# Half-row projections in pairs, two-bank PSUM tiles and a new step order in a linear-attention and gated-MLP kernel

## The chip, the cores and the metric

The kernel runs on one core of a Trainium2 chip. The metric is the device time of one launch in microseconds (us). TensorE (PE) multiplies matrices into PSUM, an accumulator of 8 banks (512 float32 values in each of 128 partitions); VectorE (DVE) and ScalarE (ACT) read PSUM and write SBUF; GpSimd (POOL) works on SBUF; SP and POOL issue most of the transfers.

## The reference

Inputs are q, k and v of 8 batches, 8 heads, 576 tokens and 64 values, and a projection w_phi of 64x128. For each head:

```python
def phi(x):
    proj = np.einsum('bhsd,df->bhsf', x, w_phi)
    proj = proj - np.max(np.abs(proj), axis=-1, keepdims=True)
    return np.concatenate([np.exp(proj), np.exp(-proj)], axis=-1)
q_p, k_p = (phi(q), phi(k))
kv = np.einsum('bhsf,bhsd->bhfd', k_p, v)
z = np.sum(k_p, axis=2)
num = np.einsum('bhsf,bhfd->bhsd', q_p, kv)
den = np.einsum('bhsf,bhf->bhs', q_p, z)[..., None] + 1e-06
```

The first stage gives num / den, a 576x512 matrix x per batch. The second stage multiplies x by w_in (512x1024), applies a relu and splits the result into u and v; v is normalized along its 512 values, mixed over tokens by the 576x576 matrix w_spatial, with a bias; u times the mixed v goes through w_out (512x512) to the output.

## The kernel before, in words

**Units and steps.** The 576 tokens are cut into 512 main tokens and a tail of 64. A unit is a pair of heads over the main tokens of one batch (32 pair units), or the tails of two batches over all 8 heads (4 tail units). Either way a unit is 128 partitions by 8 blocks. The Python loop at the end runs 40 steps for 36 units. In each step it emits, in the order of the table ORDER, pieces of first-stage work for units of different age (LAGS): keys of this step's unit, queries of the same one, attention of the unit three steps back, sums of the unit two back, and so on. After each piece, `fill(share)` adds RATE x share to a credit (in us of matmul) and takes as many second-stage tasks from a queue as the credit allows. What is left in the queue after the last step is emitted at the end. The tasks of a batch enter the queue when its last pair unit has passed the piece "out". Transfers are placed in the same loop, by unit numbers. Each engine runs its own instructions in the order they were given; waits are put in by the framework, also between two engines that read one PSUM bank.

**Projections.** `kT` and `qT` hold two blocks of 64 rows each, one under the other in 128 partitions. `wphi2` is a block-diagonal 128x256 matrix of two copies of w_phi and zeros, so `by_token` (L229 to L234) projects both blocks by one matmul of 256 columns, two of them to a PSUM bank. `a_keys` (L236) takes the maximum of the absolute values over each bank on VectorE (L244), then two exponentials of 512 columns on ScalarE (L247), with signs plus and minus; the maxima are applied by `a_scale`, which scales v on POOL (L272). `a_queries` (L249) takes maxima (L258) and splits them into a high and a low bf16 part in columns 0 to 15 of a 128x128 tile (L261, L262).

**Features.** `a_max_t` transposes that tile (L293, L294). `a_qfeat` (L296) projects the queries again, with the features on the partitions (L304 for pair units, L313 for tails), and subtracts each token's maximum by an accumulating matmul with a selector (L308, L315); two exponentials per bank follow (L321).

**Sums and numerators.** `a_kv` (L334, L336) multiplies key features by scaled v for two heads into one bank, which ScalarE or VectorE copies (L339). `a_num` (L354) multiplies query features by these sums into two banks; VectorE takes a reciprocal (L344) and multiplies (L345). `tail_num` (L382) does it for the tails in tiles of 64 columns.

**Second stage.** Tasks of four or five matmuls of 512 columns into one bank: v (L403, read by L405 on ScalarE and L406 on VectorE), u (L456, read by L458), the spatial mix (L477 and L478, read by L480 on VectorE), the output (L500, read by L502), and forms of them for the tails (L468, L489, L491).

**PSUM.** One pool of eight one-bank tiles serves everything: `psum = ... tile_pool(name="psum", bufs=8, ...)` at L57.

Of the kernel before, what the change touches and what calls it, by code (L numbers as in the profile page):

```python
# [8 lines left out]
FP32 = mybir.dt.float32  # L9
# [7 lines left out]
def kernel(  # L17
# [15 lines left out]
    nc = tc.nc  # L33
# [23 lines left out]
    psum = ctx.enter_context(tc.tile_pool(name="psum", bufs=8, space=bass.MemoryType.PSUM))  # L57
# [66 lines left out]
    wphi2 = cpool.tile([P, 2 * F], BF16)  # L124
    pin(nc.vector.memset)(wphi2, 0.0)
# [14 lines left out]
    sel1 = cpool.tile([P, H], BF16)  # L140
    sel = cpool.tile([P, H, F], BF16)
    pin(nc.vector.tensor_tensor)(out=sel1, in0=ident[:, 0:H], in1=ident[:, H:2 * H], op=ALU.add)
    pin(nc.vector.tensor_scalar)(out=sel, in0=sel1.unsqueeze(2).to_broadcast([P, H, F]), scalar1=-1.0,
# [4 lines left out]
    for i in range(2):  # L148
# [3 lines left out]
        if i == 0:  # L152
            for y in range(2):
                r = slice(y * D, (y + 1) * D)
                pin(nc.scalar.copy)(out=wphi2[r, y * F:(y + 1) * F], in_=wphi_f[r, :])
# [73 lines left out]
    def by_token(xT, half):  # L229
        ps = psum.tile([P, 4, F], FP32, tag="bank", name="ps")  # L230
        for x in range(2):
            nc.tensor.matmul(out=ps[:, 2 * x:2 * x + 2, :], lhsT=xT[:, 2 * half + x, :], rhs=wphi2,  # L232
                             start=True, stop=True)
        return ps  # L234

    def a_keys(u):  # L236

        u["mk"] = small.tile([P, H], FP32, tag="mk", name="mk")
        u["kf"] = feat.tile([P, 2, H, F], BF16, tag="kf" if u["pair"] else "kf_t", name="kf",
                            bufs=4 if u["pair"] else 2)  # L240
        for half in range(2):
            pk = by_token(u["kT"], half)
            hs = slice(4 * half, 4 * half + 4)
            nc.vector.tensor_reduce(out=u["mk"][:, hs], in_=pk, axis=AX.X, op=ALU.max,  # L244
                                    apply_absolute_value=True)
            for s, sc in ((0, 1.0), (1, -1.0)):
                nc.scalar.activation(out=u["kf"][:, s, hs, :], in_=pk, func=AF.Exp, bias=0.0, scale=sc)  # L247

    def a_queries(u):  # L249

        m, early = mhl[u["i"] % NM], u["i"] < EARLY
        if not early:
            mq = small.tile([P, H], FP32, tag="mq", name="mq")
        for half in range(2):
            pq = by_token(u["qT"], half)
            if early and half == 0:
                mq = pq[:, 0, 0:H]
            nc.vector.tensor_reduce(out=mq[:, 4 * half:4 * half + 4], in_=pq, axis=AX.X, op=ALU.max,  # L258
                                    apply_absolute_value=True)
        eng = nc.vector if early else nc.gpsimd  # L260
        eng.tensor_copy(out=m[:, 0:H], in_=mq)  # L261
        eng.tensor_tensor(out=m[:, H:2 * H], in0=mq, in1=m[:, 0:H], op=ALU.subtract)  # L262
# [28 lines left out]
    def a_max_t(u):  # L291
        pt = psum.tile([P, P], BF16, tag="bank", name="pt")
        nc.tensor.transpose(out=pt, in_=mhl[u["i"] % NM], identity=ident)  # L293
        nc.vector.tensor_copy(out=mT[u["i"] % NM][0:2 * H, :], in_=pt[0:2 * H, :])  # L294

    def a_qfeat(u):  # L296

        m = mT[u["i"] % NM]
        u["qf"] = []
        for half in range(2):  # L300
            pq = psum.tile([P, 4, P], FP32, tag="bank", name="pq")
            if u["pair"]:
                for par in range(2):
                    nc.tensor.matmul(out=pq[:, 2 * par:2 * par + 2, :], lhsT=wphi2[:, par * F:(par + 1) * F],  # L304
                                     rhs=u["qT"][:, 2 * half:2 * half + 2, :], start=True, stop=False)
                    for x in range(2):
                        j = 4 * half + 2 * x + par
                        nc.tensor.matmul(out=pq[:, 2 * par + x, :], lhsT=sel[:, j, :], rhs=m,  # L308
                                         start=False, stop=(x == 1))
# [374 lines left out]
```

## Time and profile before

| What | Value |
|---|---|
| median of 3 runs | 292.17 us (291.98 to 296.22) |
| span of the profiled execution, first to last instruction | 286.4 us |
| PE busy | 261.6 us, 91% |
| ACT busy | 229.3 us, 80% |
| DVE busy | 201.8 us, 70% |
| POOL busy | 182.2 us, 64% |
| TensorE clock granted | full throughout |
| HBM | 32.85 MB read, 9.44 MB written |

The profiled execution has no time of its own beside its span; the runs' median is 5.8 us above it, for what lies before the first and after the last instruction. The costliest groups are the exponentials of the keys (144 of 128x512, mean 692 ns) and of the features (128 for pairs, 675 ns), the scaling of v on POOL (64, 1049 ns), and the maxima of keys and queries (72 and 62 on VectorE, some 680 ns). A mean counts an instruction from start to end; where an engine starts the next one before the last has ended, starts lie closer together than that.

In the listings that follow, a line of the timeline has the start in us, the length of the run of like instructions in us, the engine, the line of the kernel, what is written and read, the tile of the array (rows*columns), the shape and the count. A line of the table by stretch has from:to, the length, the busy us and the count of each engine, the granted clock, the share of the DMA engines and GB/s.

### The profile page before, as it was taken

Reading aid. Unit: us, or ns where it says so; the run is one execution under the profiler, and the core shown is the slowest. Engines: PE = TensorE matmul, PEld = TensorE weight load, DVE = VectorE, ACT = ScalarE, POOL = GpSimd, SP = SyncE. Lnnn points to the kernel's source line nnn. Section 1 sums busy time; section 2 is a strip of 40 time slices with the busy share of each in tenths; the row PEclk is TensorE's granted clock in tenths of the full one; section 3 lists DMA queues with packets and bytes.
Section 4 is the critical chain, followed back from the end, with each engine's and each line's share of the span. In section 5 each row is a group of like instructions: output and inputs, shape, how many; then the busy total and the mean of one; then the engine's idle time right before and its main releaser. Section 6 shows DMA issues by size and latency. Waiting matters only on the chain.

```text
span 286.4 us, 7965 instructions
## 1 busy us (share of the span) xinstructions
PE 261.6 (91%) x3070; PEld 178.6 (62%) x3070; DVE 201.8 (70%) x509; ACT 229.3 (80%) x517; POOL 182.2 (64%) x320
## 2 busy tenths in 40 slices
PE   1378889999999999999989999999999999999983
PEld 1157776777666776767557687666667676545441
DVE  4389997977958877598696887578688864354610
ACT  4949998899799988999998679799999746566033
POOL 8159998798336899479689954835969600058200
PEclk9999999999999999999999999999999999999999
DMA  6989999976568499999955994999111003500037
GB/s 185 203 171 120 206 219 223 163 203 71 79 147 186 102 187 155 173 245 196 130 94 102 225 191 87 264 287 255 32 22 32 7 2 122 211 3 0 0 90 242
DMA packets 81706, 40.31 MB, mean 141 GB/s; under 512 B 50242, under 2 KB 77058, under 8 KB 81668
## 3 DMA queue, kind: packets, MB, share of 16 engines
q1 hardware_dynamic: 54180, 28.32, 43.0%
q0 software_dynamic: 27328, 11.41, 35.5%
q8 instruction: 24, 0.39, 0.6%
q14 instruction: 14, 0.11, 0.2%
q10 hardware_dynamic: 160, 0.07, 0.1%
HBM read 32.85 MB, written 9.44 MB: 148 GB/s over the span
## 4 chain that ended last, share of the span: by engine, by line
PE 61%; ACT 14%; DVE 11%; DMA 9%; POOL 2%; issue 2%; ACTq 0%; SPq 0%; POOLq 0%; DVEq 0%
PE pv L403 10%; PE ps L477 8%; PE po L500 7%; PE pu L456 7%; PE ps L232 5%; ACT qf L321 5%; ACT kf L247 5%; PE pv L334 4%; DMA q_tl<-in_q_dram 4%; PE pn L354 4%; DMA out_dram<-ob 3%; PE pq L308 3%; PE pq L304 3%; DVE mk L244 3%; PE ps L478 2%; DVE mq L258 2%
## 5 line engine op out<-in xcount | busy, mean ns | idle before, releaser
L247 ACT ACTIVATE kf<-ps 128x512 bf16<-128x512 f32 x144 | 77.7, 692 | 5.6 <-DVE mk L244 5.4
L272 POOL TENSOR_TENSOR vs<-v_f,em 128x512 bf16<-128x512 f32 x64 | 65.6, 1049 | 23.6 <-ACT em L267 22.6
L321 ACT ACTIVATE qf<-pq 128x512 bf16<-128x512 f32 x128 | 68.2, 675 | 8.5 <-PE pq L308 8.5
L244 DVE TENSOR_REDUCE mk<-ps 128x4 f32<-128x512 f32 x72 | 46.1, 677 | 2.5 <-PE ps L232 2.0
L258 DVE TENSOR_REDUCE mq<-ps 128x4 f32<-128x512 f32 x62 | 39.9, 681 | 4.2 <-PE ps L232 3.4
L502 ACT COPY ob<-po 128x512 f32<-128x512 f32 (+1 forms) x37 | 21.6, 610 | 19.9 <-PE po L500 16.2
L406 DVE BATCH_NORM_STATS2 stats<-vr 128x6 f32<-128x512 bf16 (+1 forms) x37 | 24.8, 687 | 15.8 <-ACT vr L405 15.7
L477 PE MATMUL ps<-w_spT,vn 128*128 128x512 bf16 x128 | 32.8, 379 | 0.0
L456 PE MATMUL pu<-xT,w_in_bf 128*128 128x512 bf16 x128 | 31.6, 379 | 0.0
L403 PE MATMUL pv<-w_in_bf,xT 128*128 128x512 bf16 x128 | 31.2, 379 | 0.0
L480 DVE TENSOR_TENSOR uT<-ps,uT 128x512 bf16<-128x512 f32 x32 | 22.0, 689 | 12.7 <-PE ps L478 11.5
L500 PE MATMUL po<-w_out_bf,uT 128*128 128x512 bf16 x128 | 30.4, 379 | 0.0
L308 PE MATMUL pq<-mT,sel 128*128 128x128 bf16 x256 | 30.0, 219 | 0.0
L308 PEld LDWEIGHTS <-sel 128*128 128x128 bf16 x256 | 25.1, 98 | 3.9
L405 ACT ACTIVATE vr<-pv 128x512 bf16<-128x512 f32 (+1 forms) x37 | 23.3, 691 | 4.0 <-PE pv L403 3.9
L354 PEld LDWEIGHTS <-qf 128*128 128x128 bf16 x512 | 20.4, 97 | 8.2 <-issue 1.7
L345 DVE TENSOR_TENSOR x<-pn,rc 128x256 bf16<-128x256 f32 x64 | 25.0, 418 | 0.5
L420 POOL TENSOR_SCALAR vn<-vr,rs 128x512 bf16<-128x512 bf16 x32 | 24.3, 773 | 0.8
L334 PE MATMUL pv<-vs,kf 128*128 128x66 bf16 x512 | 24.5, 194 | 0.2 <-ACT kf L247 0.2
L354 PE MATMUL pn<-kv,qf 128*128 128x66 bf16 x512 | 22.3, 193 | 1.3 <-ACT qf L321 1.2
L334 PEld LDWEIGHTS <-kf 128*128 128x128 bf16 x512 | 21.7, 97 | 1.8 <-issue 0.9
L304 PE MATMUL pq<-qT_b,wphi 128*128 128x256 bf16 x96 | 22.4, 273 | 0.0
(120 smaller groups left out, 530.8 us busy)
## 6 DMA issues: line engine op xcount, KB each, us to landing
v_f<-in_v_dram SPq DMA_DIRECT2D x8, 1024.0 KB, 10.7
out_dram<-ob SPq DMA_DIRECT2D x32, 256.0 KB, 3.6
k_bf<-in_k_dram POOLq DMA_DIRECT2D x7, 512.0 KB, 7.0
q_bf<-in_q_dram POOLq DMA_DIRECT2D x7, 512.0 KB, 8.7
v_tl<-in_v_dram SPq DMA_DIRECT2D x8, 128.0 KB, 7.7
w_in_bf<-in_moe_w_in_dram POOLq DMA_DIRECT2D x2, 512.0 KB, 8.7
out_dram<-ob SPq DMA_DIRECT2D x8, 128.0 KB, 2.4
k_tl<-in_k_dram POOLq DMA_DIRECT2D x8, 64.0 KB, 6.8
```

What stands on the lines that cost most here:

```text
L244: nc.vector.tensor_reduce(out=u["mk"][:, hs], in_=pk, axis=AX.X, op=ALU.max, apply_absolute_value=True)
L247: nc.scalar.activation(out=u["kf"][:, s, hs, :], in_=pk, func=AF.Exp, bias=0.0, scale=sc)
L258: nc.vector.tensor_reduce(out=mq[:, 4 * half:4 * half + 4], in_=pq, axis=AX.X, op=ALU.max, apply_absolute_value=True)
L272: nc.gpsimd.tensor_tensor(out=vs[:, s, :, 0:D], in0=st[u["b"]]["v"][:, pj * H:(pj + 1) * H, :], in1=em[:, s, :].unsqueeze(2).to_broadcast( ...
L308: nc.tensor.matmul(out=pq[:, 2 * par + x, :], lhsT=sel[:, j, :], rhs=m, start=False, stop=(x == 1))
L321: nc.scalar.activation(out=qf[:, s], in_=pq, func=AF.Exp, bias=0.0, scale=sc)
L334: nc.tensor.matmul(out=pv[:, hh, s, :], lhsT=u["kf"][:, s, 4 * hh + c, :], rhs=u["vs"][:, s, 4 * hh + c, :], start=(c == 0), stop=False)
L354: nc.tensor.matmul(out=pn[:, pos, :], lhsT=u["qf"][hh][:, s, pos, :], rhs=d["kv"][:, 2 * u["pj"] + hh, s, :], start=(s == 0), stop=(s == 1))
L403: nc.tensor.matmul(out=pv[r], lhsT=lhs(kc), rhs=w_in_bf[:, kc, HALF:DFF], start=(kc == 0), stop=(kc == KC - 1))
L456: nc.tensor.matmul(out=pu, lhsT=w_in_bf[:, kc, dc * P:(dc + 1) * P], rhs=d["xT"][:, kc, :], start=(kc == 0), stop=(kc == KC - 1))
L477: nc.tensor.matmul(out=ps, lhsT=d["vn"][:, sp, cs], rhs=w_spT[:, sp, 0:T0], start=(sp == 0), stop=False)
L500: nc.tensor.matmul(out=po[r], lhsT=lhs(dc), rhs=w_out_bf[:, dc, :], start=(dc == 0), stop=(dc == KC - 1))
```

## The change

PSUM is divided: a pool `wide` of two tiles of two banks, for keys and features, and a pool `psum` of four banks for everything else. The block-diagonal matrix is replaced by `wphi`, with w_phi in rows 0 to 63 and again in rows 64 to 127. Each projection is a matmul on 64 rows and 128 columns, emitted in pairs: the upper half to one bank, the lower half to the other. The blocks of a unit therefore stand in another order, which `slot` gives to the readers. Keys take one maximum over 1024 columns and two exponentials of 1024. Features take one pair of 512-column matmuls, then four pairs for the maxima; the maxima of the two halves are put into columns 0 to 7 and 64 to 71, and the selector has a copy for each half. The transposed maxima are copied on all 128 partitions. ORDER and RATE change: nothing is filled in between keys and queries, more after queries, sums and features; 3.7 us of matmul a step instead of 3.12.

```diff
-    psum = ctx.enter_context(tc.tile_pool(name="psum", bufs=8, space=bass.MemoryType.PSUM))
+    wide = ctx.enter_context(tc.tile_pool(name="wide", bufs=2, space=bass.MemoryType.PSUM))
+    psum = ctx.enter_context(tc.tile_pool(name="psum", bufs=4, space=bass.MemoryType.PSUM))
...
-    wphi2 = cpool.tile([P, 2 * F], BF16)
-    pin(nc.vector.memset)(wphi2, 0.0)
+    wphi = cpool.tile([P, F], BF16)
...
-    sel1 = cpool.tile([P, H], BF16)
-    sel = cpool.tile([P, H, F], BF16)
-    pin(nc.vector.tensor_tensor)(out=sel1, in0=ident[:, 0:H], in1=ident[:, H:2 * H], op=ALU.add)
-    pin(nc.vector.tensor_scalar)(out=sel, in0=sel1.unsqueeze(2).to_broadcast([P, H, F]), scalar1=-1.0,
+    sel1 = cpool.tile([P, 4], BF16)
+    sel = cpool.tile([P, 4, F], BF16)
+    pin(nc.vector.tensor_tensor)(out=sel1, in0=ident[:, 0:4], in1=ident[:, 4:8], op=ALU.add)
+    for i in (D, D + 4):
+        pin(nc.vector.tensor_tensor)(out=sel1, in0=sel1, in1=ident[:, i:i + 4], op=ALU.add)
+    pin(nc.vector.tensor_scalar)(out=sel, in0=sel1.unsqueeze(2).to_broadcast([P, 4, F]), scalar1=-1.0,
...
-    def by_token(xT, half):
-        ps = psum.tile([P, 4, F], FP32, tag="bank", name="ps")
-        for x in range(2):
-            nc.tensor.matmul(out=ps[:, 2 * x:2 * x + 2, :], lhsT=xT[:, 2 * half + x, :], rhs=wphi2,
-                             start=True, stop=True)
-        return ps
+    HALVES = (slice(0, D), slice(D, P))
+
+    def slot(u, hh, c):
+        return (4 * (c % 2) + 2 * hh + c // 2) if u["pair"] else (4 * (hh % 2) + hh // 2)
+
+    def by_token(xT, outs):
+        for y in range(4):
+            for par, r in enumerate(HALVES):
+                nc.tensor.matmul(out=outs[par][:, y, :], lhsT=xT[r, y, :], rhs=wphi[r, :], start=True, stop=True)
...
-        for half in range(2):
-            pk = by_token(u["kT"], half)
-            hs = slice(4 * half, 4 * half + 4)
-            nc.vector.tensor_reduce(out=u["mk"][:, hs], in_=pk, axis=AX.X, op=ALU.max,
-                                    apply_absolute_value=True)
-            for s, sc in ((0, 1.0), (1, -1.0)):
-                nc.scalar.activation(out=u["kf"][:, s, hs, :], in_=pk, func=AF.Exp, bias=0.0, scale=sc)
+        pk = wide.tile([P, 2, 4, F], FP32, tag="wide", name="pk")
+        by_token(u["kT"], [pk[:, 0], pk[:, 1]])
+        nc.vector.tensor_reduce(out=u["mk"].rearrange("p (y par) -> p par y", par=2), in_=pk, axis=AX.X, op=ALU.max,
+                                apply_absolute_value=True)
+        for s, sc in ((0, 1.0), (1, -1.0)):
+            nc.scalar.activation(out=u["kf"][:, s].rearrange("p n f -> p (n f)"),
+                                 in_=pk.rearrange("p a y f -> p (a y f)"), func=AF.Exp, bias=0.0, scale=sc)
...
-        for half in range(2):
-            pq = by_token(u["qT"], half)
-            if early and half == 0:
-                mq = pq[:, 0, 0:H]
-            nc.vector.tensor_reduce(out=mq[:, 4 * half:4 * half + 4], in_=pq, axis=AX.X, op=ALU.max,
+        pq = [psum.tile([P, 4, F], FP32, tag="bank", name="ps") for par in range(2)]
+        mq = pq[0][:, 0, 0:H] if early else small.tile([P, H], FP32, tag="mq", name="mq")
+        by_token(u["qT"], pq)
+        for par in range(2):
+            nc.vector.tensor_reduce(out=mq[:, 4 * par:4 * par + 4], in_=pq[par], axis=AX.X, op=ALU.max,
                                     apply_absolute_value=True)
         eng = nc.vector if early else nc.gpsimd
-        eng.tensor_copy(out=m[:, 0:H], in_=mq)
-        eng.tensor_tensor(out=m[:, H:2 * H], in0=mq, in1=m[:, 0:H], op=ALU.subtract)
+        m = m.rearrange("p (par n) -> p par n", par=2)
+        mq = mq.rearrange("p (par n) -> p par n", par=2)
+        eng.tensor_copy(out=m[:, :, 0:4], in_=mq)
+        eng.tensor_tensor(out=m[:, :, 4:8], in0=mq, in1=m[:, :, 0:4], op=ALU.subtract)
...
-        nc.vector.tensor_copy(out=mT[u["i"] % NM][0:2 * H, :], in_=pt[0:2 * H, :])
+        nc.vector.tensor_copy(out=mT[u["i"] % NM], in_=pt)
...
+        pq = wide.tile([P, 2, 4, P], FP32, tag="wide", name="pq")
+        for par, r in enumerate(HALVES):
+            nc.tensor.matmul(out=pq[:, par], lhsT=wphi[r, :], rhs=u["qT"][r], start=True, stop=False)
+        for y in range(4):
+            for par, r in enumerate(HALVES):
+                nc.tensor.matmul(out=pq[:, par, y, :], lhsT=sel[r, y, :], rhs=m[r, :], start=False, stop=(y == 3))
+        qf = feat.tile([P, 2, 8, P], BF16, tag="qf" if u["pair"] else "qf_t", name="qf", bufs=3 if u["pair"] else 2)
+        for s, sc in ((0, 1.0), (1, -1.0)):
+            nc.scalar.activation(out=qf[:, s].rearrange("p n t -> p (n t)"), in_=pq.rearrange("p a y t -> p (a y t)"),
+                                 func=AF.Exp, bias=0.0, scale=sc)
+        u["qf"] = qf
...
-                    nc.tensor.matmul(out=pv[:, hh, s, :], lhsT=u["kf"][:, s, 4 * hh + c, :],
+                    nc.tensor.matmul(out=pv[:, hh, s, :], lhsT=u["kf"][:, s, slot(u, hh, c), :],
...
-    ORDER = (("keys", 0.375), ("queries", 0.25), ("attention", 0), ("sums", 0.25),
-             ("next", 0.125), ("features", 0), ("out", 0), ("maxima", 0))
-    RATE = 3.12
+    ORDER = (("keys", 0), ("queries", 0.45), ("attention", 0), ("sums", 0.3),
+             ("next", 0), ("features", 0.25), ("out", 0), ("maxima", 0))
+    RATE = 3.7
```

The old body of `a_qfeat` (L300 to L322 of the kernel before) goes; `a_kv`, `a_num` and `tail_num` read the features through `slot` in the same way as the one line shown.

## The prediction

> **What bounds the kernel now.** I read the page's busy shares first, then the busy time by stretch, then the order of time on TensorE, and last the waits.
>
> ```profile
> span 286.4 us, 7965 instructions
> PE 261.6 (91%) x3070; PEld 178.6 (62%) x3070; DVE 201.8 (70%) x509; ACT 229.3 (80%) x517; POOL 182.2 (64%) x320
> PE 61%; ACT 14%; DVE 11%; DMA 9%; POOL 2%; issue 2%; ACTq 0%; SPq 0%; POOLq 0%; DVEq 0%
> ```
>
> The second line is busy time by engine, the third the chain that ended last: TensorE leads both. By stretch (columns: PE, its weight loads, DVE, ACT, POOL):
>
> ```profile
> 15.00:47.00 32.00, 27.27 (x398) 22.54 (x398) 30.23 (x86) 27.71 (x68) 28.22 (x44) 1.00 1.14 186
> 47.00:247.00 200.00, 196.52 (x2443) 137.24 (x2444) 150.49 (x374) 174.91 (x407) 133.73 (x240) 1.00 0.83 141
> 247.00:286.40 39.40, 34.18 (x210) 16.64 (x208) 14.62 (x29) 16.75 (x29) 12.28 (x22) 1.00 0.24 81
> ```
>
> Before 47 us VectorE is the full engine (30.2 of 32 us). From 47 to 247 us it is TensorE (196.5 of 200). After 247 us TensorE drains what is left of the second stage, back to back. Busy matmul time can hide gaps, since their ends are modelled, so I looked at starts:
>
> ```profile
> 220.90 0.27 PE L304 MATMUL pq<-qT_b,wphi 128*128 128x256 bf16 x1
> 221.01 0.28 PE L308 MATMUL pq<-mT,sel 128*128 128x128 bf16 x2
> 221.12 0.27 PE L304 MATMUL pq<-qT_b,wphi 128*128 128x256 bf16 x1
> ...
> 221.79 0.22 PE L293 MATMUL pt<-ident,mhl 128*128 128x128 bf16 x1
> 221.84 0.60 PE L232 MATMUL ps<-wphi,kT_b 128*128 128x256 bf16 x4
> 222.28 0.38 PE L477 MATMUL ps<-w_spT,vn 128*128 128x512 bf16 x1
> ```
>
> Starts follow one another at the rate of the columns: 0.11 us for 256, 0.055 for 128. A whole feature block takes 221.79 - 220.90 = 0.89 us, a projection block 222.28 - 221.84 = 0.44. All waits of matmuls in the middle stretch sum to 3.7 us, so TensorE issues without pause there: a us of matmul removed is a us gained, as long as no new wait appears.
>
> **What the skill says.** "TensorEngine Tiling (Array Packing)", Key Properties and Gotcha 1: tiles on different row halves run at the same time; a change of tiling mode drains TensorE; two row tiles may not write one PSUM bank at once. The trace agrees on the first two, with other shapes:
>
> ```profile
> 53.57 0.39 PE L192 MATMUL pt<-ident,wsp 128*128 128x128 bf16 x4
> 53.89 0.22 PE L194 MATMUL pt<-ident,wspt 64*128 64x64 bf16 x1
> 54.04 0.41 PE L192 MATMUL pt<-ident,wsp 128*128 128x128 bf16 x4
> ...
> 130.54 0.66 PE L354 MATMUL pn<-kv,qf 128*128 128x66 bf16 x16
> 131.13 0.72 PE L382 MATMUL pn<-kv,qf_t 128*64 128x66 bf16 x32
> 131.79 0.39 PE L456 MATMUL pu<-xT,w_in_bf 128*128 128x512 bf16 x1
> ```
>
> Four 128-column matmuls need 4 x 0.056 = 0.22 us, but the 64-row one starts 0.32 after them: 0.10 lost, and about as much on the way back. A switch costs **0.095 us**. Column tiles: 32 matmuls in 0.66 less one switch, 0.018 each, against 0.59 less one switch over 16, 0.031 each: they do overlap. Row pairs no run shows yet; the change puts their halves in two banks, as the page asks. "TensorE: Matmul & The Clock Gate", Part 3, gives about 4 ns between starts in a pack; I take 6 ns, so an N=128 pair is 0.062 us and an N=512 pair 0.222. "PSUM — Partial Sum Buffer", section on bank collisions: two engines may not touch one bank at once, two readers neither. The trace agrees: key exponentials waited 5.4 us for the maxima that read the same bank.
>
> **The change, part by part.** One step handles one unit; between 47 and 247 us lie 28 units' maxima, 30 units' features, 32 steps of 6.25 us.
>
> (1) Projections. Before: keys and queries 0.44 each (0.434 by the column rate). After: 4 pairs each, 0.248. Saved 28 x 2 x 0.186 = 10.4 us. Bounds: 0.224 with perfect overlap (11.8), 0.434 with none (0).
>
> (2) Features. Before 0.884. After one N=512 pair and four N=128 pairs, 0.222 + 0.248 = 0.470. Saved 30 x 0.414 = 12.4 us; bounds 0 and 13.1.
>
> (3) Mode switches. Keys and queries are now neighbours (share 0 after keys), so a step has four: into keys, out of queries, into and out of features (the transpose of the maxima lies between features and the next keys). 4 x 0.095 x 30 = 11.4 us on the path. Net of (1) to (3): **-11.4 us**.
>
> (4) Exponentials 1024 wide. Back to back, 512 columns start 0.478 to 0.490 apart; 264 columns (kv copy) 0.26; slope about 0.85 ns a column, so 1024 cost about 0.91. Four a unit: 3.64 against 3.9. ScalarE gains 0.25 us a step; it is 175 of 200 us busy, not the bound: worth nothing directly. Lower bound of its worth zero, upper what bursts delay.
>
> (5) Maxima. Keys: one reduce of 1024, 1.13 us (two of 0.60 less one fixed part of 0.07) up to 1.20. Queries unchanged. Gain 0.07 x 6 units in the VectorE-bound start, 0.4 us at most; the two more adds for the selector and the strided copies give some of it back. The copy of the transposed maxima grows from 16 to 128 partitions at the same 128 columns: 0.20 either way. I count the start as 0, +-1. No DMA is moved on SP's or POOL's queue.
>
> (6) More second stage a step (RATE 3.12 to 3.7). Tasks move from after the last step into steps. What must remain after it is the last batch, whose tasks are queued only then: by their matmuls and 0.216 us for 512 columns about 26 us (16 v and 16 u, 40 spatial, 32 output matmuls and the tails), against 39.4 now. The move is neutral, since TensorE is full in both places: steps grow 0.4 us, the end shrinks 13.
>
> (7) PSUM. This is the unknown. Before, 8 banks served all. Now keys and features own four and everything else (queries 2, numerators 2, sums 1, maxima 1, some four second-stage tasks) shares four. From the starts of first matmuls and the ends of last readers in the trace, a key bank lives 3.5 us, a feature bank 2.4, a query bank 1.6, numerators 1.7, v and u 3.0 to 3.4, s 2.1, o 2.7. Summed over 200 us, 2.8 banks are held by the second group on average, and above four for a sixth of the time. So the cover is thin. I worked one step by hand, from t = 0 at the keys. Keys and queries are issued by 0.64 (two switches). VectorE: key maximum 0.57 to 1.70, query maxima to 2.30 and 2.90. Two tasks on TensorE until 2.37. ScalarE: two wide exponentials from 1.75 to 3.57, the small ones to 3.76, only then the tasks' evictions, 4.25 and 4.73. The numerators take the query banks: the first at 2.40, the second at 3.00 instead of 2.66. The sums take the bank of the first numerator, normalized at 3.36: start 3.46. From there nothing is late. Lost: 0.34 + 0.20 = **0.54 us a step**. Where the tasks are spatial matmuls (VectorE evicts), the same working gives 0.27 with two in the first fill, 0.74 with one. Queued behind that wait are all matmuls, TensorE being in order; who waits for them is ScalarE's kv copy and the features, both with slack. With banks free early in some steps I take 0.45 x 32 = **+14.4 us**; bounds 0 and 0.85 x 32 = 27.
>
> Sum against the profiled execution: 286.4 - 11.4 + 14.4 = 289.4. The median 292.17 lies 5.8 above the span (start and end outside it): **295.2 us**, say 295, 1% slower.
>
> **Rivals.** *A, banks suffice*: the shared banks turn over fast enough and the order (1.67 us of tasks between queries and numerators) hides the maxima. 286.4 - 11.4 = 275 plus up to 0.17 a step; about 281 us, 4% faster. For it: 2.8 of 4 banks on average, and ScalarE's burst, 4.1 us today (features and keys adjacent), is now cut in two. Against: in-order evictions behind an exponential pair.
>
> *B, slower*: the second-stage evictions stand behind the key exponentials, which stand behind the 1.13 us maximum; a sum that gets a task's bank, not a numerator's, starts at 4.35 instead of 2.95. Price 0.75 or more a step: 286.4 - 11.4 + 24 = 299, **305 us**. It decides from 0.54 us a step on (17.2 us, where 2% is passed). For it: u's banks already wait 2 us for ScalarE. Against: that is with longer bursts.
>
> *C, the pairs don't overlap*: nothing is saved in (1) and (2), switches remain, a slower TensorE hides most waits: 286.4 + 11.4 + 5 = 303, **309 us**. Column tiles speak against it.
>
> **Chances.** 2% is about what a measurement of this kernel can tell from no change: 286.3 to 298.0. Forecast 0.37 (stall of 0.17 to 0.54 a step), A 0.29, B 0.26, C 0.08. Faster 0.29, same 0.37, slower 0.34. The range leaves out a tenth on each side: 279 to 308, from A with perfect overlap to C.
>
> **What would show it.** Keys plus queries: eight pairs within 0.5 us; features within 0.48; 0.095 beside each. Step right on (7): matmul waits of numerators and sums on query maxima, normalizations or evictions, some 14 us in all against 3.7; step near 6.7 us, steps over by 262 us of span, 27 us of drain behind. Wrong if these waits are absent (A), if they name second-stage evictions and exceed 17 us (B), or if starts in a pair are 0.055 apart (C). A DMA transpose arriving late would be a cause I have not priced.

## The result, and the profile after

The changed kernel takes 306.39 us in the median of 4 runs (304.51 to 308.16), the kernel before 294.20 (291.98 to 297.30) in the runs beside it: a ratio of 1.053 [1.044, 1.063]. Every ratio here is taken from fast runs alone, those within 1.5% of the fastest of their kernel, so that it can differ from the quotient of the medians (1.041 here): 306.39/1.053 is 291 us for the kernel before, which in the rounds of the experiments took 289.5 to 291.1 in the median. The changed kernel is 5% slower; the prediction said 295, 1% slower. The time lies inside the range and near rival B, but B's mechanism is only part of it. The profiled execution has a span of 304.2 us against 286.4: **17.8 us** to explain. Each profiled execution with a time of its own took 1.8 us more than its span, so that of the kernel before took about 288.2, below the four runs beside it and near the fast end of the later ones (from 287.25); of its 5.8 us to the median, which the prediction called start and end, some 4.0 are scatter. Differences of spans therefore come out some 2 us larger than the ratios make them (5.3% of 291 is 15.4).

The page of the changed kernel, its first lines and the chain that ended last:

```profile
span 304.2 us, 8124 instructions
PE 263.3 (87%) x3233; PEld 156.2 (51%) x3270; DVE 200.8 (66%) x474; ACT 223.4 (73%) x372; POOL 182.5 (60%) x320
PE 53%; ACT 14%; DVE 13%; POOL 8%; DMA 6%; issue 4%; ACTq 0%; DVEq 0%; POOLq 0%
```

TensorE's share of the chain fell from 61% to 53%: it waits more, and DVE, POOL and issue have taken the room. By stretch of the changed kernel (columns as before):

```profile
47.00:150.00 103.00, 95.06 (x1235) 57.14 (x1247) 74.64 (x176) 85.61 (x148) 69.86 (x125) 0.96 0.88 145
150.00:270.00 120.00, 112.22 (x1418) 65.47 (x1436) 80.76 (x188) 92.57 (x157) 67.60 (x124) 0.99 0.66 119
270.00:304.20 34.20, 27.75 (x181) 13.85 (x181) 11.64 (x22) 12.45 (x21) 10.36 (x18) 0.96 0.21 70
```

The steps run to about 271 us instead of 247, the end shrinks from 39.4 to about 33. The granted clock, full before in these stretches, is 0.96 and 0.99. The order of time on TensorE in a good place:

```profile
212.45 0.39 PE L304 MATMUL pq<-qT_b,wphi 64*128 64x512 bf16 x2
212.67 0.39 PE L307 MATMUL pq<-mT,sel 64*128 64x128 bf16 x8
212.99 0.40 PE L385 MATMUL pt<-ident,xt 128*128 128x128 bf16 x4
```

The pairs overlap: a feature block runs from 212.45 to 212.99, 0.54 us with one switch of 0.095, so 0.445 where the prediction said 0.470 and the old block took 0.89. And in a bad place:

```profile
206.31 0.39 PE L304 MATMUL pq<-qT,wphi 64*128 64x512 bf16 x2
206.54 0.39 PE L307 MATMUL pq<-mT,sel 64*128 64x128 bf16 x8
206.81 0.21 PE L237 MATMUL pk<-wphi,kT_b 64*128 64x128 bf16 x1
206.96 0.42 PE L344 MATMUL pn<-kv,qf 128*128 128x66 bf16 x8
207.31 0.34 PE L237 MATMUL pk<-wphi,kT_b 64*128 64x128 bf16 x5
207.58 0.42 PE L344 MATMUL pn<-kv,qf 128*128 128x66 bf16 x8
207.93 0.71 PE L372 MATMUL pn<-kv,qf 128*64 128x66 bf16 x32
```

One key matmul, eight numerators, five key matmuls, eight numerators: the framework does not keep the order of the program (kernels that are made to keep it follow below), and cuts blocks of half-row matmuls in pieces. Each border costs a switch. Between 47 and 270 us there are 214 switches; the old kernel had 31 up to 247 us. Of the waits of matmuls in that stretch the longest are:

```profile
PE pk L237 <- ACT kf L249: 2.5, 5, 0.9
PE pn L344 <- ACT qf L310: 1.5, 2, 0.8
PE po L490 <- DVE uTt L485: 1.4, 1, 1.4
PE pq L304 <- ACT kf L249: 1.4, 1, 1.4
PE pv L324 <- POOL vs L277: 1.1, 1, 1.1
PE pv L393 <- DVE xTt L387: 1.1, 3, 0.5
PE pv L393 <- ACT vr L395: 1.0, 2, 0.6
```

No single one stands out: keys and features wait for exponentials (their two wide tiles), second-stage tiles for evictions, tail tasks for their copies.

To count all of it, I compared the start of every matmul with the start of the one before plus its columns at the full clock (0.216 us for 512) and 0.095 for a change of tile shape; what is left over is a wait; in a stretch of granted clock 0.5 it is counted apart, waits and low clock together. Gaps where a record is missing from the trace (an exact double step inside one block) are left out. From 47 to 270 us:

| | before | after |
|---|---|---|
| switches | 31 (2.9 us) | 214 (20.3 us) |
| waits | 5.8 us | 19.0 us |
| left over at clock 0.5 | 0 | 5.75 us |

With the 22.8 us that steps (1) and (2) save, this gives -22.8 + 17.4 + 13.2 + 5.75 = +13.6. Another 4.0 us are lost early: of the 36 copies of transposed maxima (one a unit, L294 and L297), the eighth starts at 57.1 us before and at 61.1 after. Sum 17.6 of 17.8. That it comes out so well is partly luck: 22.8 is the predicted saving, for the units of the middle alone, and the early loss overlaps the stretch from 47 us. The same count over the whole traces, each matmul with its measured start, has no such freedom: columns -27.9 us, switches +20.2 (213 more), waits and low clock together +5.0 before 47 us, +19.2 from there to 270 and +1.0 behind, which makes the +17.5 us by which the last matmul starts later.

The clock may have a part in the early loss, though no run separates it. In the first 20.5 us of the kernel before the matmuls start at half the rate (four of 256 columns take 0.85 us from 15.70 to 16.55, and 0.44 later), so the clock was not full throughout. In the changed kernel this lasts to 28.7 us and returns from 35.6 to 39.0; split_alone and pairs_alone, two kernels of the next section, have a second stretch of the kind too (from 22.1 and 35.4 us). It can't be the whole of it: split_narrow, another one, has none from 23.7 us to that copy, and its eighth copy is 3.5 us late.

### The profile page after: what moved, and what is told of

Read it like the earlier page. It is cut to its first block, busy times and chain, and to the rows that moved or that the text cites. A ratio compares the mean times of both kernels' runs of the same rounds, so it can differ in the third digit from the quotient of the medians.

```text
span 304.2 us, 8124 instructions
## 1 busy us (share of the span) xinstructions
PE 263.3 (87%) x3233; PEld 156.2 (51%) x3270; DVE 200.8 (66%) x474; ACT 223.4 (73%) x372; POOL 182.5 (60%) x320
## 4 chain that ended last, share of the span: by engine, by line
PE 53%; ACT 14%; DVE 13%; POOL 8%; DMA 6%; issue 4%; ACTq 0%; DVEq 0%; POOLq 0%
PE po L490 9%; PE pv L393 8%; PE ps L467 7%; PE pu L446 5%; ACT qf L310 5%; PE pv L324 5%; DVE mk L246 4%; ACT kf L249 4%; PE pn L344 4%; DMA q_tl<-in_q_dram 4%; PE pq L304 3%; PE pq L307 2%; DMA out_dram<-ob 2%; DVE uT L470 2%; DVE mq L259 2%
## 5 line engine op out<-in xcount | busy, mean ns | idle before, releaser
L249 ACT ACTIVATE kf<-pk 128x1024 bf16<-128x1024 f32 x72 | 70.0, 1025 | 20.3 <-DVE mk L246 20.0
L310 ACT ACTIVATE qf<-pq 128x1024 bf16<-128x1024 f32 x72 | 70.5, 1031 | 13.8 <-PE pq L307 13.7
L246 DVE TENSOR_REDUCE mk<-pk 128x8 f32<-128x1024 f32 x36 | 43.9, 1220 | 3.6 <-PE pk L237 2.9
L344 PEld LDWEIGHTS <-qf 128*128 128x128 bf16 x512 | 21.6, 99 | 17.7 <-issue 6.3
L344 PE MATMUL pn<-kv,qf 128*128 128x66 bf16 x512 | 25.8, 196 | 5.2 <-ACT qf L310 4.3
L324 PE MATMUL pv<-vs,kf 128*128 128x66 bf16 x512 | 26.0, 198 | 1.3 <-POOL vs L277 1.1
L395 ACT ACTIVATE vr<-pv 128x512 bf16<-128x512 f32 (+1 forms) x37 | 21.4, 613 | 6.9 <-PE pv L393 5.6
L264 POOL CAST mhl<-mq 128x8 bf16<-128x8 f32 x31 | 6.0, 194 | 28.9 <-DVE mq L259 28.8
L326 PE MATMUL pv<-vst,kf 128*128 128x66 bf16 x128 | 22.1, 196 | 1.0 <-POOL vst L292 1.0
L290 POOL TENSOR_TENSOR vst<-v_tl,em 64x512 bf16<-64x512 f32 x16 | 16.4, 1044 | 10.0 <-ACT em L270 9.7
```

What stands on the lines that cost most here:

```text
L246: nc.vector.tensor_reduce(out=u["mk"].rearrange("p (y par) -> p par y", par=2), in_=pk, axis=AX.X, op=ALU.max, apply_absolute_value=True)
L249: nc.scalar.activation(out=u["kf"][:, s].rearrange("p n f -> p (n f)"), in_=pk.rearrange("p a y f -> p (a y f)"), func=AF.Exp, bias=0.0, s ...
L310: nc.scalar.activation(out=qf[:, s].rearrange("p n t -> p (n t)"), in_=pq.rearrange("p a y t -> p (a y t)"), func=AF.Exp, bias=0.0, scale=sc)
L324: nc.tensor.matmul(out=pv[:, hh, s, :], lhsT=u["kf"][:, s, slot(u, hh, c), :], rhs=u["vs"][:, s, 4 * hh + c, :], start=(c == 0), stop=False)
L344: nc.tensor.matmul(out=pn[:, pos, :], lhsT=u["qf"][:, s, slot(u, hh, POS[pos]), :], rhs=d["kv"][:, 2 * u["pj"] + hh, s, :], start=(s == 0) ...
```

## The experiments

The change has three parts that can be had alone: **pairs** (half-row matmuls), **split** (four banks for keys and features in two-bank tiles with wide exponentials, four shared), **order** (ORDER and RATE). All eight combinations were timed in the end; the other kernels look into parts. Ratios are against the kernel before, with 95% intervals, beside the medians of all runs; spans are of one profiled execution each.

### Each part alone, and pairs with order

split_alone, the kernel before with this edit:

```diff
-    psum = ctx.enter_context(tc.tile_pool(name="psum", bufs=8, space=bass.MemoryType.PSUM))
+    wide = ctx.enter_context(tc.tile_pool(name="wide", bufs=2, space=bass.MemoryType.PSUM))
+    psum = ctx.enter_context(tc.tile_pool(name="psum", bufs=4, space=bass.MemoryType.PSUM))
...
+        pk = wide.tile([P, 2, 4, F], FP32, tag="wide", name="pk")
...
+        pw = wide.tile([P, 2, 4, P], FP32, tag="wide", name="pq")
```

> The kernel before with one part of the change: PSUM divided into two tiles of two banks (keys, features; one maximum and two exponentials of 1024) and four shared banks. Projections stay on full rows, ORDER and RATE stay. Theory 1 (the four shared banks make TensorE wait): 15 to 25 us slower than before, 307 to 317 us, with waits of matmuls in the middle stretch of some 15 us or more against 3.7. Theory 2 (the loss comes from the changes of tiling mode and from blocks cut in pieces, not from the banks): within 4 us of before, 288 to 296 us.

Measured: 299.14 us, 1.035 [1.027, 1.042], span 298.2, between the two theories. Waits of the middle 14.5 us against 5.8. They are short and many; in the list of waits the largest stand before weight loads, and the last line is the first of them in the kernel before:

```profile
PEld L355 <- issue: 3.2, 11, 0.7
PEld L404 <- issue: 2.3, 6, 0.6
PEld L457 <- issue: 1.4, 4, 0.5
```

```profile
PEld L354 <- issue: 1.3, 4, 0.4
```

L355 (before: L354) are numerators, L404 and L457 first matmuls of second-stage tiles: the users of the shared banks. "Issue" means that the profile shows nothing they waited for, so these lines give the place and not the cause. By the count of starts 4.2 of the 14.5 us stand before numerators and 2.8 before sums (0.7 and 0.5 in the kernel before), and 3.3 before v and u.

order_alone, the kernel before with the new ORDER and RATE and nothing else:

```diff
-    ORDER = (("keys", 0.375), ("queries", 0.25), ("attention", 0), ("sums", 0.25),
-             ("next", 0.125), ("features", 0), ("out", 0), ("maxima", 0))
-    RATE = 3.12
+    ORDER = (("keys", 0), ("queries", 0.45), ("attention", 0), ("sums", 0.3),
+             ("next", 0), ("features", 0.25), ("out", 0), ("maxima", 0))
+    RATE = 3.7
```

> The kernel before with ORDER and RATE of the changed one, nothing else. Theory 1 and theory 2: TensorE is full in both places, so 290 to 296 us. Theory 3 (the new order itself costs, since keys and queries next to each other pile up 2.4 us of maxima on VectorE): 298 us or more.

Measured: 302.08 us, 1.045 [1.038, 1.051], span 300.4. The part that was counted as neutral costs the most. Waits 16.9 us, and 2.0 left over in 3.4 us of half clock. Its longest waits of matmuls between 47 and 265 us:

```profile
PE po L500 <- DVE uTt L495: 5.1, 3, 1.9
PE pv L334 <- POOL vs L274: 2.2, 1, 2.2
PE pv L403 <- DVE xTt L397: 2.0, 4, 0.5
```

pairs_alone is the changed kernel with one pool of eight single banks, 512-wide exponentials, and the old ORDER and RATE; pairs_and_order is the same with the new ones:

```diff
-    wide = ctx.enter_context(tc.tile_pool(name="wide", bufs=2, space=bass.MemoryType.PSUM))
-    psum = ctx.enter_context(tc.tile_pool(name="psum", bufs=4, space=bass.MemoryType.PSUM))
+    psum = ctx.enter_context(tc.tile_pool(name="psum", bufs=8, space=bass.MemoryType.PSUM))
...
-        pk = wide.tile([P, 2, 4, F], FP32, tag="wide", name="pk")
+        pk = [psum.tile([P, 4, F], FP32, tag="bank", name="pk") for par in range(2)]
...
-        pq = wide.tile([P, 2, 4, P], FP32, tag="wide", name="pq")
+        pq = [psum.tile([P, 4, P], FP32, tag="bank", name="pq") for par in range(2)]
```

> The kernel before with half-row pairs alone: eight single banks, exponentials of 512, ORDER and RATE of before. Emitted are 104 runs of half-row matmuls, 208 switches, 19.8 us, against 22.8 us saved. Theory 1: 287 to 292 us. Theory 2: 300 us or more, because cut blocks lose their pairs as well.

> The changed kernel with one pool of eight single banks again (keys and features in two banks each, maxima and exponentials of 512); half-row pairs and the new ORDER and RATE stay. Emitted are 78 runs of half-row matmuls, so 156 switches at 0.095 us, 14.8 us, against 22.8 us saved by the pairs in the middle. Theory 1 (banks): the stalls go, 284 to 288 us, faster than before. Theory 2 (switches and cut blocks): only the 21 runs less than in the changed kernel are gained, 4 us, 300 to 303 us.

Measured: pairs_alone 289.66 us, 0.996 [0.993, 1.000], span 288.2; pairs_and_order 300.56 us, 1.042 [1.036, 1.048], span 299.2. Alone, the pairs are worth 0.4%, not the 11.4 us of the prediction.

### What of the split costs, and what of the order

split_narrow divides the banks the same way, but leaves tiles and exponentials as they were:

```diff
-    psum = ctx.enter_context(tc.tile_pool(name="psum", bufs=8, space=bass.MemoryType.PSUM))
+    kfp = ctx.enter_context(tc.tile_pool(name="kfp", bufs=4, space=bass.MemoryType.PSUM))
+    psum = ctx.enter_context(tc.tile_pool(name="psum", bufs=4, space=bass.MemoryType.PSUM))
```

> The kernel before with the eight banks divided into four for keys and features and four for the rest, but in tiles of one bank, with maxima and exponentials of 512 as before; ORDER and RATE of before. Theory C (four shared banks are what costs in the split): 296 to 302 us, as with the split and the wide tiles. Theory D (the wide tiles cost: a maximum of 1.2 us ahead of two exponentials, two banks held together): 289 to 293 us.

Measured: 300.62 us, 1.035 [1.031, 1.039], as much as with wide tiles. The division costs; wide tiles and wide exponentials neither add nor take away. Nor do the SBUF tiles of the features, of which split_narrow keeps the seven of before, while split_alone and the changed kernel have three of double size.

rate_alone (`RATE = 3.7` only), shares_alone (the new ORDER at 3.12), and after_rate312 (the changed kernel at 3.12):

> The kernel before with RATE 3.7 instead of 3.12 and nothing else. Theory A (at 3.7 the queue of second-stage tasks runs empty at each batch, so that steps without any second-stage work follow, and first tasks stand right behind what they need): all of the loss of the new order is here, 299 to 304 us, with waits of matmuls on uTt, xTt and vs of some 10 us. Theory B (keys and queries next to each other, so that the maxima pile up): 288 to 294 us.

> The kernel before with the new shares (nothing between keys and queries, 0.45 after queries, 0.3 after sums, 0.25 after features) and RATE 3.12. Theory E (larger portions of tasks in one place: tasks that need each other's result stand side by side, behind 2.4 us of maxima on VectorE): 295 to 299 us, with waits of output matmuls on uTt. Theory F (all of the loss of the new order that is not RATE's comes from both together): 289 to 293 us.

> The changed kernel with RATE 3.12, the new shares kept. Theory A: 9 to 12 us less than the changed kernel, 294 to 298 us. Theory B: no change, 303 us or more.

Measured: rate_alone 296.85 us, 1.022 [1.015, 1.029]; shares_alone 301.99, 1.045 [1.036, 1.054]; after_rate312 314.93, 1.081 [1.074, 1.089]. Both parts of the order cost, the shares more than either of their theories had, and going back to 3.12 makes the changed kernel worse, with other waits: 8.2 us of matmuls behind the output copies on ScalarE, which themselves wait for output transfers.

What the rate does can be read from where second-stage matmuls stand in the order of time. In the kernel before, no stretch without one is longer than 5.6 us after 50 us; in rate_alone one is 14.7 us (from 130.1 to 144.9), in order_alone 14.5, in the changed kernel 13.2. The queue has run dry before the next batch's tasks arrive; at 3.12 with the new shares (shares_alone) the longest is 4.9. The changed kernel there:

```profile
138.03 0.40 PE L237 MATMUL pk<-wphi,kT_b 64*128 64x128 bf16 x8
138.26 0.48 PE L237 MATMUL ps<-wphi,qT_b 64*128 64x128 bf16 x8
139.56 0.24 PE L344 MATMUL pn<-kv,qf 128*128 128x66 bf16 x2 [0.82 <-ACT qf L310]
140.47 0.61 PE L344 MATMUL pn<-kv,qf 128*128 128x66 bf16 x14 [0.68 <-ACT qf L310]
...
143.41 0.63 PE L237 MATMUL ps<-wphi,qT_b 64*128 64x128 bf16 x8
145.10 0.38 PE L324 MATMUL pv<-vs,kf 128*128 128x66 bf16 x4 [1.06 <-POOL vs L277]
```

Between queries and numerators, where the prediction put 1.67 us of tasks as cover, nothing stands; the exponentials and POOL's scaling come to the surface. And the clock follows (changed kernel, by stretch of 3.4 us):

```profile
134.58:138.00 3.42, 3.27 (x53) 2.18 (x51) 3.15 (x7) 2.53 (x6) 2.89 (x8) 1.00 0.75 225
138.00:141.40 3.40, 1.90 (x55) 1.48 (x56) 3.11 (x7) 3.40 (x6) 3.33 (x5) 1.00 0.69 130
141.40:144.80 3.40, 2.64 (x47) 1.82 (x42) 2.81 (x9) 2.95 (x5) 3.08 (x4) 0.50 0.93 109
144.80:148.20 3.40, 2.77 (x34) 1.83 (x33) 1.57 (x4) 1.83 (x4) 3.05 (x9) 0.50 1.49 197
148.20:151.60 3.40, 3.00 (x7) 1.19 (x9) 0.13 (x1) 2.92 (x6) 2.20 (x3) 0.50 1.35 191
```

After 3.4 us in which TensorE was busy for 1.90, the granted clock is one half for 10.2 us. What is left over there are the 5.75 us of the count; half a clock can have cost at most half of the 10.2, 5.1 us, and the rest are waits. order_tails_late asked whether the wait for uTt is the cost of the order: order_alone with the tail's v and output tasks queued later.

```diff
-        if tail:
-            ts.append((mm, lambda: b_v_tail(g, bls)))
         ts += [(mm, lambda j=j: b_v(b, j)) for j in range(NB)]
+        if tail:
+            ts.append((mm, lambda: b_v_tail(g, bls)))
```

> The kernel before with the new ORDER and RATE, and with the tail tasks moved in the list of a batch: v of the tails after the normalization of v, the output of the tails after the outputs of the main tokens, so that neither stands right behind what it needs. Theory E: the waits on uTt and xTt go, 6 us less than with the new order alone, 294 to 297 us. Theory F, or steps without tasks as the whole cause: 299 us or more.

Measured: 304.17 us, 1.051 [1.044, 1.059]. The waits for uTt and xTt are gone, others take their place (spatial matmuls on POOL's vnt 3.1 us, sums on POOL's vs 2.3). The named wait was not the cost.

Four kernels then took the new ORDER apart at rate 3.12. adjacent_only moves one share; shares_keysfill fills behind sums and features as the new order does, but keeps keys and queries apart:

```diff
+    ORDER = (("keys", 0), ("queries", 0.625), ("attention", 0), ("sums", 0.25),
+             ("next", 0.125), ("features", 0), ("out", 0), ("maxima", 0))
```

```diff
+    ORDER = (("keys", 0.2), ("queries", 0.25), ("attention", 0), ("sums", 0.3),
+             ("next", 0), ("features", 0.25), ("out", 0), ("maxima", 0))
```

> The kernel before, rate 3.12, with one edit of the order: the share after keys (0.375) goes to the place after queries (0.625), everything else as it was. If the cost of the new order comes from keys and queries standing side by side (their maxima pile up on VectorE, the queries reach for transposed data sooner): 3 to 5% slower, 300 to 305 us. If it comes from the shares moved behind sums and features: within 1%, 291 to 294 us.

> The kernel before, rate 3.12, with shares 0.2 after keys, 0.25 after queries, 0.3 after sums, 0 after next, 0.25 after features: tasks stand behind sums and features as in the new order, but keys and queries stay apart. If adjacency is the cause: within 1.5%, 291 to 295 us. If the place behind sums and features is the cause: 3 to 5% slower, 300 to 305 us.

Measured: adjacent_only 304.24 us, 1.042 [1.033, 1.051]; shares_keysfill 301.79, 1.036 [1.027, 1.046]. Each theory was to exonerate one half; both halves cost about 4%. Matmuls wait for the queries that a DMA transposes, and ScalarE's output copies for output transfers. In shares_keysfill, matmuls first, then ScalarE:

```profile
PE ps L232 <- DMA qT_b<-q_bf: 4.5, 2, 2.6
PE pn L382 <- ACT ob L502: 2.9, 1, 2.9
```

```profile
ACT ob L502 <- DMA out_dram<-ob: 5.7, 4, 2.7
```

The kernel before has 1.4 us of the first and 1.7 of the last. shares_xp3 and adjacent_xp3 place these transposes one step earlier (`XP = 3` instead of 2) in shares_alone and adjacent_only:

> The kernel before with the new shares at rate 3.12, and the transposes of keys and queries by DMA placed one step earlier. Without that edit this order waited 4.3 us for transposed keys and queries (key and query matmuls) and 5.1 us on ScalarE for output transfers. If late transposes are what the shares cost: those waits go and the time falls from 302 to 294-297 us. If they only mark a place where something else is late (the output transfers on the same queue, maxima): 300 us or more.

> The kernel before at rate 3.12, the share after keys moved behind queries, and the transposes by DMA placed one step earlier. Without that edit: 304 us, 7.8 us of waits for transposed keys and queries, 13.4 us on ScalarE for output transfers. If late transposes are the cause: 294 to 298 us. If the time hangs on the output transfers or on the order itself: 301 us or more.

Measured: shares_xp3 301.81 us, 1.037 [1.027, 1.047]; adjacent_xp3 298.95, 1.030 [1.023, 1.037]. In adjacent_xp3 no matmul waits for transposed queries any more, and a third of the loss may be gone (1.042 to 1.030, the intervals overlap); ScalarE still waits 10.2 us for output transfers, and one wait of a weight load on the transposed x (L403) is 6.2 us. The late transposes are a part at most.

### Combinations

pairs_and_split is the changed kernel with the old ORDER and RATE, split_and_order is split_alone with the new ones.

> The changed kernel with the old step order and rate: half-row pairs, two-bank tiles for keys and features, four shared banks. If the parts add up (pairs -0.4%, split +3.5%): 3% slower, about 300 us, and the new order then costs the changed kernel another 2% (306 us with it). If the pairs and the split get in each other's way (half-row matmuls need both halves' banks at once): 5% or more, 306 us, and the order costs nothing on top of them, as step 6 of the prediction had it.

> The kernel before with the two-bank tiles, four shared banks, the new order and rate 3.7, but no pairs. If the two costs add (split 3.5%, order 4.5%): 8%, about 314 us, so that the pairs are worth some 2.5% in the changed kernel, more than on their own. If the split and the order lose the same time (both are waits of the same matmuls): 5%, 306 us, and the pairs are worth nothing there either.

Measured: pairs_and_split 300.02 us, 1.036 [1.030, 1.043], span 299.1; split_and_order 303.09 us, 1.047 [1.041, 1.054], span 300.7. The whole table:

| | old order | new order |
|---|---|---|
| 8 banks, full rows | 1 (286.4) | 1.045 (300.4) |
| 8 banks, pairs | 0.996 (288.2) | 1.042 (299.2) |
| split, full rows | 1.035 (298.2) | 1.047 (300.7) |
| split, pairs | 1.036 (299.1) | 1.053 (304.2) |

Down each pair of rows the **pairs** do nothing: -0.4% and +0.2% with the old order, -0.3% and +0.6% with the new one. **Split and order don't add**: 3.5 and 4.5 alone, 4.7 together. Where the removed matmul time went shows from the same count as above, us of the stretch from 47 to 270:

| pairs added to | blocks (predicted) | switches more | waits and low clock more | eighth copy later | sum | span |
|---|---|---|---|---|---|---|
| nothing | -22.8 | 169, +16.1 | +5.9 | +3.2 | +2.4 | +1.8 |
| split | -22.8 | 218, +20.7 | +0.8 | +1.3 | 0.0 | +0.9 |
| order | -22.8 | 117, +11.1 | +10.8 | +0.2 | -0.7 | -1.2 |
| both | -22.8 | 177, +16.8 | +6.0 | +2.7 | +2.7 | +3.5 |

Where there are fewer switches there are more waits. Over the whole traces the same count takes 26.1 to 27.7 us of columns out in each of the four, puts 13.7 to 23.6 us of switches in, and leaves the rest to waits and low clock. In pairs_and_order no block is cut (72 runs of half-row matmuls in the trace, as many as the program has): its 117 switches more are about the 120 of the prediction, and there waits took the rest.

### Fewer switches

If cut blocks are the loss, keeping blocks whole should help. after_pinned and pairs_pinned keep all matmuls in the order the program gives them (72 runs of half-row matmuls in their traces, against 113 in the changed kernel and 99 in pairs_alone), by giving each one the edit below; pairs_pinned is pairs_alone with this and the new shares at 3.12. pairs_merged is pairs_alone at 3.12 with a step order that puts features, keys and queries side by side, and tail tasks late (40 runs).

```diff
-            nc.tensor.matmul(out=pq[:, par], lhsT=wphi[r, :], rhs=u["qT"][r], start=True, stop=False)
+            pin(nc.tensor.matmul)(out=pq[:, par], lhsT=wphi[r, :], rhs=u["qT"][r], start=True, stop=False)
```

```diff
+    ORDER = (("keys", 0), ("queries", 0.5), ("attention", 0), ("sums", 0.3),
+             ("next", 0.2), ("maxima", 0), ("out", 0), ("features", 0))
```

> The changed kernel with every matmul kept in the order of the program, so that no block is cut: 72 runs of half-row matmuls instead of 99 to 106, some 60 switches less, 5 to 6 us. Theory G: 299 to 302 us. Rival: what was moved ahead filled a wait, and the wait comes back, 306 us or more.

> Half-row pairs with eight single banks, exponentials of 512, the new shares (keys and queries next to each other) with RATE 3.12, and every matmul kept in the order of the program, so that no block is cut: 72 runs of half-row matmuls, 144 switches, 13.7 us. Theory A: 22.8 us saved less 13.7, so 281 to 285 us, faster than both kernels. Theory B: 290 us or more.

> Half-row pairs with eight single banks and exponentials of 512; the maxima's transpose moved ahead of the features, so that features, keys and queries follow one another, with 0.5 of the tasks after them, 0.3 after sums and 0.2 after next; RATE 3.12; tail tasks late as above. Emitted are 40 runs of half-row matmuls: 80 switches, 7.6 us, instead of 208 and 19.8 us in the kernel with pairs alone. Theory G (switches are what eats the gain of the pairs): 12 us less than with pairs alone, 276 to 281 us, faster than both kernels. Theory H (four 512-wide exponentials of features and four of keys, with all maxima, in one pile make TensorE wait for banks): 290 us or more.

Measured: after_pinned 316.75 us, 1.095 [1.088, 1.101]; pairs_pinned 306.88, 1.056 [1.049, 1.063]; pairs_merged 310.46, 1.069 [1.057, 1.082]. The first is worse than the changed kernel, the others than pairs_alone. Only the first tests the pinning by itself: pairs_pinned has the new shares besides, which alone cost 4.5%, and pairs_merged a new step order. Waits are 40.3 us in after_pinned against 19.0 in the changed kernel. The longest (L62 is the line that pins):

```profile
PE pn L62 <- DVE mq L259: 5.8, 12, 1.6
PE po L62 <- DVE uTt L485: 5.4, 3, 2.0
```

The first is the wait of step (7), numerators behind the query maxima whose bank they take, twelve times. In the changed kernel's stretch from 47 to 270 us pinning takes 70 of 214 switches away, 6.7 us, and adds 21.3 us of waits. A reading that fits, but that no single cut was traced for: a cut costs two switches, 0.19 us, and is made where the block, or what stands behind it, would wait longer. The switch count isn't a fault to mend alone; at least in part it is the price at which waits were avoided.

## Why the prediction was wrong, step by step

- **(1), (2) Right.** A pair of 128 columns takes 0.057 us (predicted 0.062): four pairs from 138.03 to 138.26 above. A feature block 0.445 (0.470). Rival C is out.
- **(3) The step that failed first.** "Net of (1) to (3): -11.4 us" was worth between -1.2 and +3.5 us of span in four comparisons (-1.1 to +1.7 by the ratios). The price of a switch, 0.095, was right; "four a step", counted from the program's order, was not: in the changed kernel 183 more instead of 120, 17.4 us instead of 11.4 (in pairs_and_order, where no block is cut, 117). The other part of the failure is the sentence beneath it, "a us of matmul removed is a us gained, as long as no new wait appears". The condition didn't hold: 0.8 to 10.8 us of waits came up in the middle, which the removed matmuls had hidden. The trace of before gave no warning, since it shows only waits that were not hidden; what it did show, 3.7 us of waits, I read as slack.
- **(4) Right.** Two wide exponentials that follow one another take 1.82 us from the first start to that of the copy behind them (118.98 to 120.80), 0.91 each; not on the path (split_narrow costs the same without them).
- **(5) Size right, worth wrong.** The key maximum takes 1.22 us (1.13 to 1.20). But the start was "0, +-1", and the eighth unit is 4.0 us late. Split alone has 2.7 us of such a delay, pairs alone 3.2; the cause I didn't isolate, and the clock of the start was not in the sum at all.
- **(6) The step that failed outright.** "The move is neutral, since TensorE is full in both places". The new order alone costs 14.0 us of span. Where the queue runs dry TensorE isn't full (1.90 of 3.4 us), and the work moved into steps before is not there to cover waits; then the clock halves. The sum said only how much work moves, and not when a batch's tasks exist. The shares cost as much without the rate (1.045).
- **(7) Size a little high, mechanism shown in part.** The split alone: 11.8 us of span against 14.4, of it 8.7 as waits in the middle and 2.7 at the start. Of the 8.7, 5.8 stand before numerators and sums, where the step put all of them. What they wait for isn't named there; the query maxima stand by name in after_pinned (5.8 us before numerators, twelve times), and hardly in the changed kernel (0.5 us).
- **The sum.** (6) and (7) together were put at 0 + 14.4; measured 300.7 - 286.4 = 14.3. That is a coincidence of a high (7) with a zero (6) and of costs that overlap, not a confirmation. Of the 5.8 us added at the end for start and end some 4.0 were scatter; with 1.8 the forecast would have been 291.2, so that luck brought it nearer to the result. In this grouping the whole miss of the sum, 304.2 - 289.4 = 14.8 us, is the gain of the pairs that wasn't there (-11.4 against +3.5). Taken in the other order (split, then pairs, then the new order: +11.8, +0.9, +5.1) 12.3 of it is the pairs, 5.1 the order, and -2.6 the split. Every path has 10 us or more on the pairs.
- **Rivals.** B gave 305 us and asked for 17 us of waits on evictions. The waits exceed 17, but few name an eviction of the second stage; B is near by its number, not by its mechanism. A needed banks to suffice, and fails with the split alone.
- "A DMA transpose arriving late" does appear, not in the changed kernel, but at rate 3.12 for keys and queries (4.5 us in shares_keysfill), and for x in some kernels at 3.7 (3.3 us of matmuls in pairs_and_order).

**What stays open.** Why nearly every shift of the second-stage tasks costs 2 to 5%, with another waiter each time, isn't settled. The traces are consistent with a kernel in which output transfers, transposes, evictions and batch arrivals happen to miss one another, and any shift makes some meet; that was only argued. Four named waits were taken away (uTt, xTt, the rate's dry queue, late transposes), and each time most of the loss stayed. Nothing tested is clearly faster than the kernel before; pairs_alone at 0.996 [0.993, 1.000] is as good.

Two statements of the Trainium skill bear on this. "TensorEngine Tiling (Array Packing)", Key Properties, says that a change of tiling mode drains TensorE; the runs agree, and 0.095 us times the changes decided the worth of the packing. "TensorE: Matmul & The Clock Gate", Part 1, gives a window of 3413 ns and half the clock after an idle one; the low stretches here are 3.4, 6.8 and 10.2 us long, and within a trace the changes lie whole multiples of 3.41 us apart (35.56, 38.97, 141.37 and 151.61 us in the changed kernel), which fits. But windows with TensorE busy for 1.90 of 3.40 us, and in pairs_and_order for 2.48 of 3.41, were idle enough, and here the measurement decides. Nor does the busy share decide alone: on the same grid the windows from 247.2 to 250.6 in the changed kernel (1.88 busy) and from 242.3 to 245.7 in order_alone (1.53) were followed by a full clock.

## What to carry to other kernels

A busy engine at 98% isn't proof that removed work is gained: count what the removed instructions cover, by asking for each wait how long it would be if the work before it were gone. Count mode switches from the order the scheduler emits, not from the program's blocks. When work is moved between a loop and its end, check that it exists when it is wanted; a queue that ran dry here cost its idle time and then a slower clock.

## What the runs showed that I had not expected

- The second matmul of a row pair mostly starts 3 to 4 ns after the first, and a pair of N=128 costs 57 ns, hardly more than one full-row matmul (56).
- A stretch of 3.4 us with TensorE busy for 1.90, 1.23 (order_alone) or 1.19 us (rate_alone) was followed by at least 3.4 us at half clock, and others as idle (1.53, 1.88) were not.
- Keeping matmuls in program order made the changed kernel 3.4% slower (316.75 against 306.39) with fewer switches.
- Costs of 3.5% and 4.5% made 4.7% together: parts measured alone could not be added. That their waits overlap fits this, but wasn't followed wait by wait.
